# Attention with a softplus feed-forward on one core: q and k of the first three units loaded head-major and transposed in bf16

## The chip, the cores and the metric

The kernel runs on one core of one Trainium2 chip, in one launch. The metric is the device time in microseconds (us) from start to end; 218.96 us is the median of three runs of the kernel before (218.79 to 218.98). The profile is of one execution, which took 219.03 us.

## The reference

Two stages. Attention over 4 sequences of 768 tokens with 8 heads of 64; a query sees the 8 first tokens and its last 96, with a bias by distance. Then, for each of 3072 tokens, a feed-forward of 512 to 2048 to 512 with softplus.

```python
scores = scale * np.matmul(q, k.transpose(0, 1, 3, 2))
keep = is_global | is_local            # pos < 8, or 0 <= rel < 96
scores = np.where(keep, scores + bias, -1e9)
a = softmax(scores)
x = np.matmul(a, v)                    # to [tokens, heads * 64]
h = x @ w_in
g = np.maximum(h, 0.0) + np.log1p(np.exp(-np.abs(h)))
out = g @ w_out
```

## The kernel before, in words

**Tiling.** A block is 128 tokens of a sequence; a unit is two blocks (`UNITS`, L204: twelve units, twenty-four blocks). A unit's q, k and v are loaded as float32 (512 KB each), cast to bf16, and q and k are transposed so that the 64 features of a head lie on partitions. Of a block's scores, TensorE computes key tile by query (L1005 for the first block, L1058 for the others), the bias is added on TensorE (L995, L1039, for the first two blocks) or on VectorE (L1084), ScalarE exponentiates (L1018, L1091), TensorE multiplies with v and a column of ones (L1110), VectorE divides (L1121, L1122), and the result is transposed to `XT` (L1141 on TensorE for the first six blocks, by a DMA after that). Two blocks make a group of 256 tokens: `mm1` (L1168, eight slots of eight matmuls) writes h, ScalarE computes exp and ln(1+e) (L1183, L1194), `mm2` (L1217) multiplies with w_out, and `store` copies and writes out (L1246, L1249).

**The first three units** (`WIDE`, L205: units 0, 1 and 2) have a path of their own for q and k. Each of these six tensors is loaded in two DMAs of 256 KB, one for the even heads and one for the odd heads (L780 to L783): 128 partitions of 2 KB, eight tokens of one head in each. Partition number is token group times four plus head (`"h (g r) d -> g h (r d)"`). The first q is issued on ScalarE's queue (`LOAD_ON`), all other loads on SyncE's. `cast_q` (L841) casts each half, 128x512. `transp_pe` (L914 to L947) transposes on TensorE by a matmul with the identity (L926): the output is float32 in PSUM, and because heads alternate from partition to partition, each matmul scatters its 128 columns over the bank with a stride. One q or k of a unit has eight such matmuls and fills two banks. Then either one copy of 1024 columns (L939) or two of 512 (L936) bring it to bf16 in `qT` or `kTa`/`kT`. The other nine units are loaded whole (L790 to L793), and a DMA transposes them (L953).

**Weights** come in sixteen loads of 512 KB (L821), eight of w_in and eight of w_out, and are cast to bf16 (L823).

**What sets the order.** Each piece of work is an `op` with an engine, an assumed duration and a due time. `Planner.run` (L90) plays the pieces through a model of the engines and of the transfers (constants `FETCH`, `DMA_FIRST`, `DMA_LAST` and the pair `dma=(work, packet)` of an op) and fixes the order on each engine; the instructions are then written out in this order. `NUDGE` shifts due times of single ops, `CHOICE` gives the engine of an op that could run on several. So the constants do not appear in the instructions; they decide where these stand. `filler` (L1330) makes 35 matmuls on a blank tile, written where the planner sees TensorE without work. On the chip each engine goes through its list in order and waits on semaphores.

Of the kernel before, what the change touches and what calls it, by code (L numbers as in the profile page):

```python
# [23 lines left out]
class Planner:  # L24
# [5 lines left out]
    FETCH = 15.5  # L30
    FETCH_COST = 1.0
    DMA_FIRST = 0.75
# [182 lines left out]
    0: (("s", 1, 0), ("s", 1, 1), ("s", 0, 0), ("s", 0, 1)),  # L215
    1: (("s", 1, 0), ("s", 1, 1), ("s", 0, 0), ("s", 1, 0)),
    2: (("s", 0, 0), ("s", 1, 0), ("s", 1, 0), ("s", 0, 0)),
# [48 lines left out]
    "a0.0": -2,  # L266
    "a0.1": -14.5,
    "a0.2": -3,
    "a0.4": 2.25,
    "a1.0": -1,  # L270
    "a1.1": -4.25,
    "a1.2": -3.5,
    "a1.3": -0.5,
    "a1.4": 0.5,
    "a1.6": 15,
    "a1.7": -2,
    "a2.0": 8,
    "a2.2": -11,
    "a2.3": 1.5,
    "a2.4": 4,  # L280
    "a2.5": -10.25,
    "a2.6": -4,
    "a2.7": 8,
    "b0.0.2": 10.5,
    "b0.0.4": -8.5,
    "b0.0.8": -8,
    "b0.1.0": 0.5,
    "b0.1.10": -7.5,
    "b0.1.12": -14.75,
    "b0.1.14": 2.75,  # L290
    "b0.1.2": -1,
    "b0.1.4": 3.75,
    "b0.1.6": -40.75,
    "b0.1.8": 2.75,
    "b1.0.0": 4.75,
    "b1.0.10": 4.5,
    "b1.0.12": -11,
    "b1.0.14": -2,
    "b1.0.2": 1,
    "b1.0.4": -0.5,  # L300
    "b1.0.8": -18.25,
    "b1.1.0": 4.25,
    "b1.1.10": -0.5,
    "b1.1.12": 0.25,
    "b1.1.4": 0.5,
    "b1.1.6": 10,
    "b1.1.8": 55.75,
    "biasFalse0": 2.25,
    "biasFalse2": -2,
    "biasFalse4": 5.5,  # L310
    "biasFalse5": -6.75,
    "biasFalse6": 10,
    "biasFalse7": -5.25,
    "biasTrue0": 1.75,
    "biasTrue2": -2,
    "biasTrue3": 2,
    "biasTrue4": -4,
    "biasTrue6": -0.5,
    "biasTrue7": -1.5,
    "blank": -7,  # L320
    "castk0.0": -2.25,
    "castk0.1": -11.25,
    "castk1.1": 11.5,
    "castk2.0": 4,
    "castk2.1": -8.25,
    "castk3.00": 4.5,
    "castk3.01": -2.5,
    "castk3.10": -0.25,
    "castk3.11": 1,
    "castk4.00": 3.5,  # L330
    "castk4.11": -0.25,
    "castq0.1": 23.25,
    "castq1.1": 16,
    "castq2.0": -17.25,
    "castq2.1": 1.5,
    "castq3.0": 7,
    "castq5.0": 9,
    "castv0.01": 3.5,
    "castv0.10": -1.25,
    "castv0.11": 3,  # L340
    "castv1.00": -13.5,
    "castv1.01": 4,
    "castv1.10": 4,
    "castv1.11": -4.5,
    "castv2.00": 6.5,
    "castv2.01": 8,
    "castv2.10": 8.5,
    "castv2.11": 1.25,
    "castv3.00": 0.75,
    "castv3.10": 0.25,  # L350
    "castv3.11": -20,
    "castv4.00": 1,
    "castv4.10": 0.25,
    "castv4.11": -8,
    "castv6.10": -0.5,
    "castv6.11": -8,
    "cin1": -10,
    "cin2": -3.25,
    "cin3": -67.25,
    "cin4": -0.5,  # L360
    "cin5": -6,
    "cin6": -0.25,
    "cin7": 29,
    "cout0": -6.75,
    "cout1": -19.5,
    "cout3": 0.75,
    "cout4": 2.5,
    "cout6": 6,
    "cout7": -3.25,
    "cpk0.0": -2.75,  # L370
    "cpk1.0": 20.25,
    "cpk1.1": 6.75,
    "cpk2.0": -2,
    "cpk2.1": 9,
    "cpq0.0": 7.25,
    "cpq1.0": -1.25,
    "cpq2.0": 3,
    "d0": -4.25,
    "dl0a": -0.25,
    "dl0b": -0.25,  # L380
    "dl0c": -0.25,
    "dl1a": 0.5,
    "dl1e": 2.5,
    "e0.1": 3.75,
    "e0.2": -4,
    "e0.3": -18.75,
    "e0.4": -1,
    "e0.6": -0.5,
    "e1.0": -2,
    "e1.1": 2,  # L390
    "e1.2": -23,
    "e1.3": 12.5,
    "e1.5": 0.5,
    "e1.6": -1,
    "e1.7": -9.75,
    "e2.3": 2.75,
    "e2.4": -0.5,
    "e2.5": 11.25,
    "ex0.0": 0.75,
    "ex0.1": -8,  # L400
    "ex2.0": -67.75,
    "ex2.1": 2.25,
    "ex3.0": 6.5,
    "ex3.1": -1.5,
    "ex4.0": -23.5,
    "ex4.1": 3.75,
    "ex5.0": -0.25,
    "ex5.1": -26,
    "ex6.0": 0.5,
    "ex6.1": 8.5,  # L410
    "ex7.0": 23.75,
    "ex7.1": 3.75,
    "gk4": 0.5,
    "gk6": 11.75,
    "gk8": 12,
    "gv4.0": -0.75,
    "gv4.1": 1.25,
    "gv5.0": -1,
    "gv5.1": 12,
    "gv6.0": 7,  # L420
    "gv6.1": -6,
    "gv7.1": 0.25,
    "gv8.0": -8,
    "gv8.1": 1,
    "ident": 9.75,
    "iota": -1,
    "ldk0.0": -2,
    "ldk0.1": -6.25,
    "ldk1.0": -5.25,
    "ldk2.0": 0.25,  # L430
    "ldk2.1": 26,
    "ldk3": -4,
    "ldk4": 10.5,
    "ldk5": 1.75,
    "ldq0.0": 1,
    "ldq0.1": 23,
    "ldq1.1": -4,
    "ldq2.0": 12.5,
    "ldq2.1": -4.25,
    "ldq3": -4,  # L440
    "ldv0": 13,
    "ldv3": -8.75,
    "ldv4": -9.5,
    "ldv5": 4,
    "ldv6": -2,
    "ldv7": 16.75,
    "ldv8": 8,
    "ln0.0": 16.5,
    "ln0.2": 4.75,
    "ln0.3": -8.5,  # L450
    "ln1.0": -15,
    "ln1.2": 2,
    "ln2.0": -177.75,
    "ln2.1": 8.75,
    "ln2.2": -8,
    "nm1.0": -12,
    "nm2.0": 7.25,
    "nm2.1": 1,
    "nm3.0": -1,
    "nm3.1": -1,  # L460
    "nm5.0": 2,
    "nm6.0": -12,
    "nm6.1": 1,
    "oc0.0.0": 4,
    "oc0.1.0": 30.25,
    "oc1.0.0": -8,
    "pv0.0": 12,
    "pv0.1": -17.75,
    "pv1.0": -4,
    "pv1.1": 1.25,  # L470
    "pv2.0": 12,
    "pv2.1": -13.75,
    "pv3.0": 0.25,
    "pv3.1": 5.5,
    "pv4.1": 1,
    "pv5.0": -4,
    "pv5.1": 1,
    "pv6.0": 3,
    "pv6.1": -3.25,
    "sb0.0": 2.25,  # L480
    "sb1.1": 17.5,
    "sc0.0": -8,
    "sc1.0": 8,
    "sc1.1": 7.75,
    "sc2.0": 0.5,
    "sc3.0": 9,
    "sc4.0": 7.25,
    "sc5.1": 2,
    "sc6.0": 0.5,
    "sc7.0": -2.25,  # L490
    "st0.0.0": 7.25,
    "st0.1.0": -0.25,
    "st1.0.0": 1,
    "table": -3,
    "trk0.0": 1.5,
    "trk1.0": 1.5,
    "trk1.1": 72.5,
    "trk2.0": -24.5,
    "trk2.1": 1.5,
    "trk4": -2.5,  # L500
    "trq0.0": -36.5,
    "trq1.0": 2,
    "trq2.0": 4,
    "trq2.1": 0.5,
    "trq3": 0.25,
    "trq5": 0.25,
    "win1": -0.5,
    "win5": -16,
    "win6": 1,
    "wout0": -12.5,  # L510
    "wout1": -1.75,
    "wout2": -18.5,
    "wout4": 3.75,
    "wout5": 2,
    "wout7": -11.75,
    "xc1": 5.25,
    "xc2": 1,
    "xc3": 1.75,
    "xc4": 0.25,
    "xc5": -6.5,  # L520
    "xt1": 2,
    "xt2": -82.5,
    "xt4": 5.25,
    "xt5": -2,
    "xt6": -6.75,
    "z2.0": 0.25,
    "z3.0": -8.25,
    "z4.0": -2,
    "z4.1": 15,
    "z5.0": -2,  # L530
    "z6.0": 8,
    "z6.1": -47.25,
# [22 lines left out]
    "biasFalse0": "POOL",  # L555
    "biasFalse2": "DVE",
    "biasFalse5": "DVE",
    "biasTrue0": "DVE",
    "biasTrue1": "DVE",
    "biasTrue2": "DVE",  # L560
    "biasTrue3": "POOL",
# [5 lines left out]
    "castk2.0": "POOL",  # L567
    "castk3.00": "ACT",
    "castk3.01": "ACT",
    "castk3.10": "DVE",  # L570
    "castk3.11": "ACT",
    "castk4.00": "DVE",
    "castk4.01": "ACT",
    "castq0.0": "POOL",
# [3 lines left out]
    "castq4.0": "POOL",  # L578
    "castq5.0": "POOL",
    "castv0.00": "DVE",  # L580
    "castv0.01": "POOL",
    "castv0.10": "ACT",
    "castv1.00": "DVE",
    "castv1.01": "POOL",
    "castv1.10": "DVE",
    "castv2.11": "ACT",
    "castv3.00": "ACT",
    "castv3.01": "DVE",
    "castv3.10": "ACT",
    "castv3.11": "DVE",  # L590
    "castv4.01": "ACT",
    "castv4.10": "ACT",
    "castv4.11": "ACT",
    "cin1": "ACT",
    "cin3": "DVE",
    "cin5": "DVE",
    "cin6": "DVE",
    "cout3": "ACT",
    "cout6": "DVE",
    "cout7": "DVE",  # L600
    "cpk0.0": "DVE",
    "cpk1.1": "ACT",
    "cpk2.1": "DVE",
    "cpq0.0": "ACT",
    "cpq2.1": "ACT",
    "gk4": "ACT",
    "gk5": "ACT",
    "gk6": "ACT",
    "gk7": "ACT",
    "gv4.0": "ACT",  # L610
    "gv4.1": "ACT",
    "gv5.0": "ACT",
    "gv6.0": "DVE",
    "gv8.0": "DVE",
    "oc0.0.0": "ACT",
    "xc1": "ACT",
    "xc4": "ACT",
# [13 lines left out]
def kernel(  # L631
# [116 lines left out]
    def held(keys):  # L748

        return sorted({key[:2] for key in keys})  # L750
# [13 lines left out]
    def load_unit(i, rank, only="qkv"):  # L764
# [4 lines left out]
        for z, which in enumerate(only):  # L769
# [4 lines left out]
            if i in WIDE and which != "v":  # L774
                for y in range(2):

                    on = LOAD_ON.get(f"{which}{i}", "SP")

                    def fn(src=src, raw=raw, y=y, on=on):
                        return dma_on[on].dma_start(  # L780
                            raw[:, 512 * y : 512 * y + 512],
                            src[y::2, sl, :].rearrange("h (g r) d -> g h (r d)", r=8),
                        )  # L783

                    op(f"ld{which}{i}.{y}", on, 0.64, rank + 0.01 * z, fn, dma=(0.68, 86.0), sync=sync,
                       writes=[("raw", slot, y)])
                continue
# [7 lines left out]
            op(f"ld{which}{i}", "SP", 0.45, rank + 0.01 * z, fn, dma=(2.5 if (which, i) == ("v", 0) else 1.8, 30.0), sync=sync,  # L795
# [84 lines left out]
    def q_of(n):  # L880
# [3 lines left out]
        if i in WIDE:  # L884
            return lambda rows, m: t[rows, NPAIR * x + m, :]
# [5 lines left out]

    def kt_unit(i):
        name, slot = kt_tile(i)
        return {"kTa": kTa, "kT": kT}[name][slot][:]
# [605 lines left out]
```

## Time and profile before

| | |
|---|---|
| median of three runs | 218.96 us |
| profiled execution | 219.03 us, its span 217.2 us: 1.83 us lie outside the span |
| TensorE matmul (PE) busy | 211.7 us, 97% |
| ScalarE (ACT), VectorE (DVE), GpSimd (POOL) busy | 170.7, 115.7, 74.4 us |
| granted TensorE clock | 0.998 |
| DMA | 40.95 MB, mean 188 GB/s; 333 to 387 GB/s in the slices from 5 to 38 us |

The page is in parts: busy time of each engine; the span in 40 equal slices of 5.43 us, as tenths of busy time; DMA queues; the chain of work that ended last; the costliest groups of instructions, by line of the kernel; and DMA issues. In rows of a timeline the first number is the start, the second the time from the start of the row's first instruction to the end of its last, and xN counts instructions merged into the row. Matmuls overlap: the time that a run of matmuls takes from TensorE is read from the start of one row to the start of the next.

### The profile page before, as it was taken

To read this page: it belongs to the slowest core of one execution; us is meant where nothing else is said; L and a number is where in the kernel's file an instruction comes from. 1 tells how busy PE (TensorE), PEld (TensorE's weight loads), DVE (VectorE), ACT (ScalarE), POOL (GpSimd) and SP (SyncE) were. 2 spreads that over 40 slices of the span, in tenths; PEclk is the share of its full clock that TensorE was granted. 3 is DMA by queue.
4 is the path that set the end of the run, shared out by engine and by line. 5 is a ranking of instruction groups with operands and counts; after the bars stand their busy time and mean duration, and the time that the engine had idled before them with its cause. 6 is when DMAs were issued, how large, how long until landed. Compare 5 with 4: busy or idle time off the path is not lost.

```text
span 217.2 us, 4970 instructions
## 1 busy us (share of the span) xinstructions
PE 211.7 (97%) x2003; PEld 144.5 (67%) x2003; DVE 115.7 (53%) x216; ACT 170.7 (79%) x236; POOL 74.4 (34%) x127
## 2 busy tenths in 40 slices
PE   7899999999999999999999999999999999999994
PEld 2576887656665787757767767756766767767554
DVE  6568868674489667327546546446545952101121
ACT  4899999999995699978788688678697878788300
POOL 6316333253059525900265274233236320000000
PEclk9999999999999999999999999999999999999999
DMA  5999999999999399945895996892687212011112
GB/s 202 333 367 387 386 357 367 317 286 214 225 317 175 104 236 264 211 108 155 147 231 160 159 218 165 207 165 72 127 209 198 69 30 75 0 48 53 48 48 97
DMA packets 69846, 40.95 MB, mean 188 GB/s; under 512 B 30144, under 2 KB 61248, under 8 KB 69824
## 3 DMA queue, kind: packets, MB, share of 16 engines
q1 hardware_dynamic: 69392, 40.05, 72.1%
q10 hardware_dynamic: 432, 0.59, 0.9%
q8 instruction: 15, 0.25, 0.5%
q14 instruction: 7, 0.06, 0.1%
HBM read 27.26 MB, written 6.29 MB: 154 GB/s over the span
## 4 chain that ended last, share of the span: by engine, by line
PE 83%; ACT 12%; DMA 2%; issue 2%; SPq 0%; DVE 0%
PE h_ps L1168 34%; PE o_ps L1217 30%; PE s_ps L1058 5%; PE x_ps L1110 4%; ACT pb L1091 3%; ACT e L1183 3%; PE s_ps L1217 3%; PE s_ps L926 2%; DMA raw<-in_k_dram 2%; PE x_ps L1217 2%; ACT g L1194 2%; PE x_ps L1330 1%; ACT vb L976 1%; ACT XT L1146 1%; ACT kb L865 1%
## 5 line engine op out<-in xcount | busy, mean ns | idle before, releaser
L1168 PE MATMUL h_ps<-XT,w_in_bf 128*128 128x256 bf16 x768 | 95.8, 273 | 0.9 <-ACT e L1183 0.7
L1168 PEld LDWEIGHTS <-w_in_bf 128*128 128x128 bf16 x768 | 73.6, 98 | 18.7 <-issue 1.7
L1217 PE MATMUL o_ps<-w_out_bf,g 128*128 128x512 bf16 (+1 forms) x320 | 77.7, 371 | 0.0
L1183 ACT ACTIVATE e<-h_ps 128x512 f32<-128x512 f32 x96 | 59.5, 627 | 20.9 <-PE h_ps L1168 20.5
L1217 PEld LDWEIGHTS <-g 128*128 128x128 bf16 x416 | 37.3, 98 | 28.6
L1084 DVE TENSOR_TENSOR z<-s_ps,biasA 128x1024 f32<-128x1024 f32 x38 | 45.8, 1219 | 15.2 <-PE s_ps L1058 8.6
L1194 ACT ACTIVATE g<-e 128x1024 bf16<-128x1024 f32 x48 | 50.7, 1057 | 1.3
L1091 ACT ACTIVATE pb<-z 128x1024 bf16<-128x1024 f32 (+1 forms) x44 | 43.1, 988 | 7.9 <-DVE z L1084 7.9
L1246 DVE COPY osb<-o_ps 128x512 f32<-128x512 f32 (+1 forms) x20 | 13.4, 670 | 37.1 <-PE o_ps L1217 37.1
L976 POOL COPY vb<-vb 4x512 bf16<-4x512 bf16 x27 | 16.4, 608 | 33.0 <-PE x_ps L1110 28.6
L865 POOL CAST vb<-raw 64x512 bf16<-64x512 f32 x33 | 20.4, 617 | 18.0 <-DMA raw<-in_v_dram 16.8
L865 POOL CAST kb<-raw 64x512 bf16<-64x512 f32 x30 | 18.6, 619 | 19.5 <-DMA raw<-in_k_dram 18.4
L1110 PEld LDWEIGHTS <-pb 128*128 128x128 bf16 x352 | 16.5, 98 | 6.1 <-ACT pb L1091 0.2
L1122 DVE TENSOR_TENSOR xs<-x_ps,rcp 128x256 bf16<-128x256 f32 x40 | 17.0, 424 | 1.4
L1121 DVE RECIPROCAL rcp<-x_ps 128x4 f32<-128x4 f32 x40 | 7.2, 179 | 18.7 <-PE x_ps L1110 18.3
L1110 PE MATMUL x_ps<-vb,pb 128*128 128x65 bf16 x304 | 15.9, 193 | 0.0
L1217 PE MATMUL s_ps<-w_out_bf,g 128*128 128x512 bf16 (+1 forms) x64 | 13.6, 352 | 0.0
L1330 PE MATMUL x_ps<-blank 128*128 128x512 bf16 x35 | 11.1, 442 | 1.2 <-DVE blank L1269 1.2
L1058 PEld LDWEIGHTS <-kT 64*128 64x128 bf16 x224 | 6.8, 94 | 5.1 <-issue 4.9
L1058 PE MATMUL s_ps<-qT,kT 64*128 64x128 bf16 x224 | 9.9, 218 | 0.0
L1084 DVE TENSOR_TENSOR z<-s_ps,bias 128x512 f32<-128x512 f32 x6 | 3.9, 687 | 7.3 <-PE s_ps L1058 7.3
L1246 ACT COPY osb<-x_ps 128x128 f32<-128x128 f32 x1 | 0.3, 266 | 8.7 <-PE x_ps L1217 8.7
(84 smaller groups left out, 120.7 us busy)
## 6 DMA issues: line engine op xcount, KB each, us to landing
raw<-in_v_dram SPq DMA_DIRECT2D x12, 512.0 KB, 5.7
out_dram<-osb SPq DMA_DIRECT2D x23, 256.0 KB, 2.3
raw<-in_q_dram SPq DMA_DIRECT2D x9, 512.0 KB, 4.5
raw<-in_k_dram SPq DMA_DIRECT2D x9, 512.0 KB, 5.6
raw<-in_moe_w_in_dram SPq DMA_DIRECT2D x8, 512.0 KB, 9.5
raw<-in_moe_w_out_dram SPq DMA_DIRECT2D x8, 512.0 KB, 8.6
raw<-in_k_dram SPq DMA_DIRECT2D x6, 256.0 KB, 6.0
raw<-in_q_dram SPq DMA_DIRECT2D x4, 256.0 KB, 8.0
```

Source lines behind the costliest of these rows:

```text
L865: copy_on[eng](dst, src)
L976: copy_on[eng](vb_of(prev)[sl, :, 0:D], vb_of(first)[sl, :, 0:D])
L1058: nc.tensor.matmul(reg if unit_of(n) in WIDE else reg.rearrange("p (r t) -> p r t", r=2), kt[rows, 2 * part + m, :], qv(rows, 2 * part + m ...
L1084: nc.vector.tensor_tensor(z, src, bias, ALU.add)
L1091: nc.scalar.activation(pb[:, 0:nr, :].rearrange("p (y a) b -> p y (a b)", y=2), src, AF.Exp, scale=1.0 / root_d)
L1110: nc.tensor.matmul(xv[:, h, :], pb[:, 4 * (h % 2) + 2 * part + h // 2 if lone else u_all * (2 * (h % 2) + h // 2) + u, :], vb_of(prev if u ...
L1122: nc.vector.tensor_tensor(xs[:, 4 * part : 4 * part + 4, :], xv[:, :, 0:D], rcp[:][:, :, None].to_broadcast([P, 4, D]), ALU.mult,)
L1168: last = nc.tensor.matmul(hv[:, j, :], w_in_bf[:, m, fb * P : fb * P + P], XT[g % NXG][:, m, :], start=(m == 0), stop=(m == NM - 1),)
L1183: nc.scalar.activation(e[:, p % 2, :, :].rearrange("p j (b t r) -> p (j b) r t", b=2, r=2), hb[:].rearrange("p (a r t) -> p a r t", a=4, r=2),
L1194: nc.scalar.activation(gt[:, 2 * p - 2 : 2 * p + 2, :].rearrange("p a t -> p (a t)"), e[:].rearrange("p a j t -> p (a j t)"), AF.Ln, bias=1.0,
L1217: nc.tensor.matmul(bank(key)[:, 0 : z - a], gt[:, fb, ns * P : ns * P + P], w_out_bf[:, fb, a:z], start=(fb == 0), stop=(fb == NFB - 1),)
L1246: copy_on[eng](osb[:, a:z], bank(key)[:, 0 : z - a])
```

## The change

**Loads.** The halves of q and k of units 0 to 2 keep their size, number and 2 KB rows; partition number is now head times 32 plus token group. On the DRAM side the outermost dimension of the transfer was 32 token groups and is now 4 heads; on the SBUF side it stays 128 partitions.

**Transposes.** Eight transposes per q or k as before, but with a bf16 result of 128 contiguous columns each, so that one q or k fills one bank and not two. They stand as one op (`PE_KEYS` names one bank, not up to four).

**Copies out.** Always two copies of 512 columns; each reads PSUM with a stride of 128 columns and writes 64 columns in a row. In `qT` and `kTa`/`kT` a wide unit's head pairs and blocks change places, which `q_of`, `kt_unit` and `globals_k` follow.

**Planner.** `FETCH` 15.5 to 18.0, `DMA_FIRST` 0.75 to 0.62, the assumed work of the first v load 2.5 to 1.8, the assumed duration of the table load 1.3 to 0.1; new `NUDGE` and `CHOICE` tables. The assumed work of a wide half (0.68) stays.

What comes of it in the instruction lists: 48 transposes, 35 fillers, 768 matmuls of `mm1` and all other matmuls are as many as before. The lists' order to the last transposes of q (unit 2) is another, but what stands ahead of them on TensorE is the same in number: 64 matmuls of mm1, 48 of L1110, 48 of scores, 16 of L1141, all fillers; ahead of them in addition, now, the eight of k of unit 2, which stood behind. SyncE's loads, before: k0 k0, v0, q1 q1, k1, w_in, k1, v1, seven w_in, q2 q2, k2 k2, three w_out, v2, four w_out, q3, k3, w_out. After: k0 k0, q1, v0, q1, w_in, k1, two w_in, k1, w_in, v1, four w_in, k2 k2, q2 q2, three w_out, v2, four w_out, q3, k3, w_out. On ScalarE's queue both halves of q0 in both.

```diff
-    FETCH = 15.5
+    FETCH = 18.0
-    DMA_FIRST = 0.75
+    DMA_FIRST = 0.62
...
 PE_KEYS = {
-    0: (("s", 1, 0), ("s", 1, 1), ("s", 0, 0), ("s", 0, 1)),
-    1: (("s", 1, 0), ("s", 1, 1), ("s", 0, 0), ("s", 1, 0)),
-    2: (("s", 0, 0), ("s", 1, 0), ("s", 1, 0), ("s", 0, 0)),
+    0: (("s", 0, 0), ("s", 1, 0)),
+    1: (("s", 1, 0), ("s", 0, 0)),
+    2: (("s", 0, 0), ("s", 1, 0)),
 }
...
                             raw[:, 512 * y : 512 * y + 512],
-                            src[y::2, sl, :].rearrange("h (g r) d -> g h (r d)", r=8),
+                            src[y::2, sl, :].rearrange("h (g r) d -> h g (r d)", r=8),
                         )
...
-            return lambda rows, m: t[rows, NPAIR * x + m, :]
+            return lambda rows, m: t[rows, 2 * m + x, :]
...
+    def kT_t(i):
+        name, slot = kt_tile(i)
+        return {"kTa": kTa, "kT": kT}[name][slot]
+
     def kt_unit(i):
-        name, slot = kt_tile(i)
-        return {"kTa": kTa, "kT": kT}[name][slot][:]
+        t = kT_t(i)[:]
+        return t.rearrange("p x m t -> p (x m) t").rearrange("p (m x) t -> p x m t", x=2) if i in WIDE else t
...
-    def transp_pe(i, which, banks, engs, rank):
+    def transp_pe(i, which, key, engs, rank):
...
+        tr = bank(key).bitcast(BF16)
+
+        def mm():
+            for r in range(2):
+                for a in range(4):
+                    c, z = P * (2 * a + r), P * (4 * r + a)
+                    nc.tensor.transpose(tr[:, z : z + P], src[:, c : c + P], ident[:])
+
+        op(f"tr{which}{i}.0", "PE", 0.45, rank, mm, count=8,
+           reads=[(which + "b", i % NQB, x) for x in range(4)] + ["ident"], writes=held([key]))
+        for r in range(2):
+
+            def ev(eng, r=r):
+                copy_on[eng](
+                    dst[:, :, 64 * r : 64 * r + 64].rearrange("p c (g a) -> p c g a", a=4),
+                    tr[:, 512 * r : 512 * r + 512].rearrange("p (a c g) -> p c g a", a=4, g=16),
+                )
...
-        dst = kt_of(prev).rearrange("p m (r t) -> p (m r) t", r=2)[:, :, 0:GH]
-        src = kt_of(first).rearrange("p m (r t) -> p (m r) t", r=2)[:, :, 0:GH]
+        dst = kt_of(prev).rearrange("p m (r t) -> p m r t", r=2)[:, :, :, 0:GH]
+        src = kt_of(first).rearrange("p m (r t) -> p m r t", r=2)[:, :, :, 0:GH]
...
-    op("table", "ACT", 1.3, TABLE_RANK, table, writes=["table"])
+    op("table", "ACT", 0.1, TABLE_RANK, table, writes=["table"])
```

## The prediction, as made before the changed kernel was run

> **What bounds the kernel now.** I read the page's busy times first, then the waits of TensorE, then its timeline. TensorE is busy 97% of the span and waits for others three times, 2.5 us in all:
>
> ```profile
> PE 211.7 (97%) x2003; PEld 144.5 (67%) x2003; DVE 115.7 (53%) x216; ACT 170.7 (79%) x236; POOL 74.4 (34%) x127
> ...
> DMA  5999999999999399945895996892687212011112
> GB/s 202 333 367 387 386 357 367 317 286 214 225 317 175 104 236 264 211 108 155 147 231 160 159 218 165 207 165 72 127 209 198 69 30 75 0 48 53 48 48 97
> ```
>
> ```profile
> PE x_ps L1330 <- DVE blank L1269: 1.2, 1, 1.2
> PE h_ps L1168 <- ACT e L1183: 0.7, 2, 0.4
> PE s_ps L926 <- ACT kb L841: 0.6, 1, 0.6
> ```
>
> So the time is TensorE's list laid end to end, plus what holds it up. That list includes 35 fillers. What the fillers cover is the wait for data: in the same stretch the transfers run flat out (DMA row: 9 of 10 from the second slice on, to 387 GB/s). An earlier end needs fewer us of TensorE work; a later end comes from data that arrive later than TensorE's list asks for them, and here the DMA has no slack to make up with.
>
> The rows of TensorE that the working uses (start, us, ..., count):
>
> ```profile
> 6.79 1.05 PE L926 MATMUL s_ps<-ident,kb 128*128 128x128 bf16 x8 [0.62 <-ACT kb L841]
> 7.63 1.08 PE L926 MATMUL s_ps<-ident,qb 128*128 128x128 bf16 x8
> ...
> 15.97 0.43 PE L1141 MATMUL h_ps<-ident,xs 128*128 128x128 bf16 x4
> 16.24 1.03 PE L1330 MATMUL x_ps<-blank 128*128 128x512 bf16 x4
> ```
>
> ```profile
> 29.24 1.04 PE L926 MATMUL s_ps<-ident,qb 128*128 128x128 bf16 x8
> ```
>
> Eight old transposes take 7.63 - 6.79 = 0.84 us of TensorE, 0.105 each. Four bf16 transposes with contiguous output (L1141) take 16.24 - 15.97 = 0.27; at the other places of that line 0.23. I use 0.0575 each. From the transposes of q of unit 2 (29.24) to the end of the span lie 217.2 - 29.24 = 187.96 us, all of it TensorE's list and its tail.
>
> The transfers, in stretches (the last two columns are the mean share of the 16 DMA engines and GB/s):
>
> ```profile
> 2.00:3.00 1.00, 1.00 (x4) 0.44 (x3) 0.88 (x4) 0.67 (x1) 0.47 (x3) 1.00 0.68 156
> 3.00:4.00 1.00, 1.00 (x4) 0.29 (x3) 0.92 (x6) 0.11 (x1) 0.31 (x2) 1.00 1.03 385
> 4.00:5.00 1.00, 1.00 (x4) 0.36 (x3) 0.90 (x6) 0.50 (x2) 0.94 (x2) 1.00 1.05 402
> ...
> 6.00:7.00 1.00, 0.38 (x4) 0.21 (x4) 0.00 (x0) 0.88 (x3) 0.20 (x1) 1.00 1.12 324
> ...
> 20.00:25.00 5.00, 4.64 (x54) 4.08 (x52) 4.47 (x10) 4.95 (x8) 1.63 (x3) 1.00 1.05 387
> ```
>
> From 3 to 4 us only halves of k0 and q0 can be in flight, and all sixteen engines are full: 385 GB/s, 24 for each engine.
>
> **The transposes and copies.** 48 transposes save 0.0475 each, 2.28 us of TensorE: 1.06 ahead of the point at 29.24 (32 old ones, 3.36, against 40 new, 2.30) and 1.22 behind it (16 old, 1.68, against 8 new, 0.46). All other matmuls and the fillers are as many on both sides of this point. Where TensorE is never short of data, all 2.28 us are gain.
>
> Copies out: two of 512 in place of one of 1024 or two of 512. The rows:
>
> ```profile
> L939 ACT CAST qT<-s_ps 128x1024 bf16<-128x1024 f32 x2 | 2.0, 1012 | 0.3 <-PE s_ps L926 0.3
> ...
> L936 DVE CAST kT<-s_ps 128x512 bf16<-128x512 f32 x2 | 1.4, 691 | 0.7 <-PE s_ps L926 0.7
> ...
> L936 ACT CAST kTa<-s_ps 128x512 bf16<-128x512 f32 x2 | 1.1, 589 | 0.0
> ...
> L1146 DVE COPY XT<-o_ps 128x512 bf16<-128x512 bf16 x2 | 0.8, 416 | 0.4 <-PE o_ps L1141 0.4
> ```
>
> A copy that reads bf16 with a stride is not in the trace. Bounds: 0.42 on DVE (contiguous bf16) and, twice the float32 row, 1.38. I take the float32 rows, 0.69 and 0.59: ACT takes 0.57 for contiguous bf16 too, and the 0.27 that DVE gains there may go with the stride. Then two copies on two engines cost about 0.7 where one of 1024 cost 1.0 to 1.2; ACT and DVE have gaps there, and fillers stand on TensorE (5 after the first transposes before, 7 now), so this is worth nothing at the end. At 1.38 it would cost 0.7 on the path of each q and k, bounded under the rivals. The moved casts and biases land on engines that, in the forecast below, wait for data anyway: nothing. The four-dimensional copies of the global keys (32 elements, about 0.2 us) and the planner's constants: nothing.
>
> **The loads: the large term.** The size, rows and issue costs stay; what changes is the outermost dimension on the DRAM side, 32 token groups before, 4 heads after. A transfer must be dealt out to sixteen engines. Every load of the kernel before has an outermost size that sixteen divides on both sides (32, or 128 for v and the weights, to 128 partitions), and the rows show all sixteen busy; none shows what happens with 4. Bounds: still sixteen engines, 262,144 B / 387 GB/s = 0.68 us a half; or one engine per head, four engines, each moving 65,536 B at 24.2 GB/s: 2.71 us. I take 2.71: dealing out whole outermost items is the simplest rule that fits the rows, and with it four items cannot occupy more than four engines. I also take it that these are the same four every time, since nothing in the code steers it.
>
> Beside this stands a rule: the Trainium skill, page "DMA: Bandwidth & Descriptors", section "Why a DMA increments its semaphore by 16 and not by 1", says that a transfer runs on the largest number of engines up to 16 that divides the slowest dimension of both sides, and on HWDGE on the lowest-numbered ones. By it 32 and 128 give 16, with which the trace agrees (385 GB/s), and 4 and 128 give 4, the forecast's case; no run so far shows the second.
>
> Then those four engines are the queue that everything passes through, because every other transfer also has a sixteenth of its bytes on each of them. Work on each of the four up to the last half of q2, in SyncE's new order: 12 halves x 2.71 = 32.5; 8 w_in of 524,288 B at 387 GB/s, 1.35 each, 10.8; v0 and v1 in 512 B rows (row 6 to 7 us, 324 GB/s), 1.62 each, 3.2. Sum 46.5 us, against 12 x 0.68 + 14.0 = 22.2 before. Start: 156 GB/s in the third us means 0.4 us at full rate, so 2.6. The last half of q2 is in at 49.1. From last byte to cast: k0a and q0a (524 KB) were moved by 3.96 (156 KB by 3.0, the rest at 385 GB/s), and the first cast of k started at 4.70: 0.74. The cast of this half stands on POOL, 0.72 (723 ns); TensorE follows 0.05 later (6.74 to 6.79). So the transposes of q2 start at 49.1 + 0.74 + 0.72 + 0.05 = 50.6.
>
> Nothing ahead of them on TensorE is later: the eighth w_in is in after 12 - 4 = 8 halves, 21.7 + 10.8 + 3.2 = 35.7, at 38.3, cast (1.12 on POOL) by 40.2, and k2 (two halves later) at 44.5. Behind them: 187.96 - 1.22 = 186.7 us. The last w_out needs 8 x 1.35 + 3 x 1.62 = 15.7 more, so 66.6 with landing and cast; TensorE's new list asks for it some 17.7 us after the transposes (68.3). It holds by under 2 us, so I add no stall, but up to 5 us above.
>
> Sum: 50.6 + 186.7 = 237.3, and 219.03 - 217.2 = 1.83 outside the span: 239.1 us. The profiled execution is 0.07 above the median, which I neglect. **Predicted: 239.1 us**, 20 us slower.
>
> **The rivals.**
>
> *Sixteen engines all the same: faster.* If the cut reaches inside a head, halves take 0.68 us. Then the list is 2.28 us shorter, and the two stalls of about 0.5 us at 21.8 and 26.75 may or may not go: 217.2 - 2.28 = 214.9, with 1.83 outside 216.8 us (215.8 without the stalls). It holds up to about 0.8 us a half: the queue then ends at 2.6 + 14.0 + 12 x 0.8 = 26.2, and with 1.5 for landing and cast q2 is there at 27.7; TensorE reaches its transposes at 29.24 - 1.06 = 28.2, or 0.5 sooner. For it: nothing in the rows excludes it, the DRAM bytes are contiguous. Against: it needs a cut within an item.
>
> *Sixteen engines, but strided copies at twice the price.* Each of unit 0 and 1's copies adds 0.7 to TensorE's start of scores, k after q on both engines: 2 x 1.4 = 2.8 beyond the fillers. 216.8 + 2.8 = 219.6, about no change or slightly slower. For: before, a stride on TensorE's own output doubled its time (0.105 against 0.0575). Against: ACT's 0.57 and 0.59 for bf16 and float32 show a price that goes by elements.
>
> *Four engines, but other ones for each transfer.* The total then spreads, only the time of one transfer grows by 2.03. Halves overlap, and units 0 and 1 are each later by about one such step: 214.9 + 2 x 2.03 + 1.83 = 220.8.
>
> **How the numbers follow.** Four common engines 0.80 (239.1); sixteen, fine 0.11 (216.8, faster); sixteen with slow copies 0.05 (219.6: slower 0.03, same 0.01, faster 0.01); four changing ones 0.04 (slower 0.03, same 0.01). Faster by over 0.2%, about what a measurement of this kernel can tell, 0.12; same 0.02; slower 0.86. The range for the first case: at 402 GB/s the queue is 1.7 us shorter, and if the four engines, alone on the memory, move up to 10% more than a sixteenth of the full rate, 5 us: 232. At 324 GB/s the queue is 9 us longer, with 5 for w_out and unit 3: 253. So 232 to 253, which with 0.80 for its case is the 8 in 10; the faster case lies outside.
>
> **What would show it.** Right: slices of the first 49 us at about 180 GB/s (8.4 MB in 46.5 us) in place of 333 to 387; halves of q and k landing far over 10 us after issue; TensorE waiting ahead of the transposes of k1 and q2, for casts that waited for DMA; the row of q2's transposes at about 50.6, eight in 0.46 us; from there on TensorE as dense as before. Wrong: 380 GB/s from 3 us on and the transposes of q2 at 27 to 29, which is the faster rival. Copies of 512 at over 1 us would show the second rival.

## The result, and the profile after

The changed kernel takes **246.43 us** (median of five runs, 245.95 to 247.14), the kernel before 218.96 (218.79 to 219.36): a ratio of 1.1257, 95% interval 1.1233 to 1.1280. The forecast was 239.1 us, 232 to 253: the side is right and the time lies in the range, but the loss is 27.5 us where 20 were forecast. The profiled execution has a span of 244.9 us, so 1.8 us lie outside it, as before. All ratios here are of fast executions; the longest execution of experiments 3 and 8 counts as slow, so it is in their medians and not in their ratios.

The page, TensorE's busy time, the granted clock and the transfers by slice (now 6.1 us each):

```profile
PE 218.7 (89%) x1974; PEld 146.8 (60%) x2003; DVE 115.7 (47%) x220; ACT 167.5 (68%) x227; POOL 79.7 (33%) x135
...
PEclk9858776995999999999999999999999999999999
...
GB/s 52 153 152 206 216 258 192 217 205 308 277 305 220 272 242 204 116 218 287 179 81 143 262 147 211 144 157 257 95 130 175 193 64 24 64 43 15 32 86 86
```

The first nine slices (55 us) move 52 to 258 GB/s, 183 on average; before, 333 to 387 stood from 5 to 38 us. The granted clock is below nine tenths in slices 2 to 7 (6 to 43 us) and in slice 10 (55 to 61 us), and nowhere else.

The windows of after, three rows (the last three columns are the granted clock, the share of the 16 DMA engines and GB/s):

```profile
5.00:6.00 1.00, 1.00 (x4) 0.44 (x3) 0.48 (x2) 0.00 (x0) 0.92 (x2) 1.00 0.26 100
...
20.00:25.00 5.00, 2.18 (x22) 0.83 (x17) 0.00 (x0) 2.03 (x5) 1.87 (x3) 0.99 0.82 217
...
55.00:60.00 5.00, 3.79 (x22) 2.90 (x23) 2.49 (x4) 4.18 (x7) 0.69 (x1) 0.50 0.82 288
```

From 5 to 6 us the first halves of q and k are moving (v0, whose issue ends at 6.99, shows from 8 us on): 0.26 of 16 is 4.2 engines, with 24 GB/s each. The same row of before, in which v0 is already moving, has 1.05 and 326 GB/s. From 20 to 25 us weights move beside the halves: 13.1 engines are busy, but with 16.5 GB/s each.

The waits of TensorE, the longest three, and its timeline around the transposes of k2 and q2:

```profile
PE h_ps L1001 <- ACT bias L1312: 5.9, 1, 5.9
PE s_ps L939 <- ACT qb L851: 5.5, 1, 5.5
PE s_ps L939 <- DVE rcp L1127: 3.5, 2, 1.9
```

```profile
49.05 0.61 PE L939 MATMUL s_ps<-ident,kb 128*128 128x128 bf16 x8 [1.62 <-DVE rcp L1127]
49.50 0.38 PE L1147 MATMUL o_ps<-ident,xs 128*128 128x128 bf16 x4
...
56.21 1.01 PE L939 MATMUL s_ps<-ident,qb 128*128 128x128 bf16 x8 [5.45 <-ACT qb L851]
57.10 3.57 PE L1174 MATMUL h_ps<-XT,w_in_bf 128*128 128x256 bf16 x16
60.60 0.29 PE L1064 MATMUL s_ps<-qT,kT 64*128 64x128 bf16 x2
```

The releasers named are on the compute engines, but the one that matters was late itself: the cast `qb` that releases the transposes at 56.21 had waited 7.78 us for `raw<-in_q_dram`. The transposes of k2 take 49.50 - 49.05 = 0.45 us, those of q2, after 5.45 us of idle TensorE, 0.89. From 57 us to the end no wait is listed: the delay is complete by then.

### The profile page after: what moved, and what is told of

Its sections match the earlier page's. It is cut to its first block, busy times and chain, and to the rows that moved or that the text cites. A ratio compares the mean times of both kernels' runs of the same rounds, so it can differ in the third digit from the quotient of the medians.

```text
span 244.9 us, 4949 instructions
## 1 busy us (share of the span) xinstructions
PE 218.7 (89%) x1974; PEld 146.8 (60%) x2003; DVE 115.7 (47%) x220; ACT 167.5 (68%) x227; POOL 79.7 (33%) x135
## 4 chain that ended last, share of the span: by engine, by line
PE 73%; DMA 14%; SPq 10%; issue 1%; DVE 0%; ACT 0%; POOL 0%; ACTq 0%; POOLq 0%
PE h_ps L1174 31%; PE o_ps L1223 26%; DMA raw<-in_q_dram 7%; SPq L790 5%; DMA raw<-in_v_dram 5%; PE s_ps L1223 5%; PE x_ps L1116 4%; PE s_ps L1064 4%; SPq L831 3%; DMA XT<-xs 2%; PE x_ps L1223 2%; SPq L800 2%; PE s_ps L939 0%; ACT qb L851 0%; POOL vb L875 0%
## 5 line engine op out<-in xcount | busy, mean ns | idle before, releaser
L1174 PE MATMUL h_ps<-XT,w_in_bf 128*128 128x256 bf16 x768 | 98.5, 278 | 0.2
L1174 PEld LDWEIGHTS <-w_in_bf 128*128 128x128 bf16 x768 | 74.4, 100 | 18.8 <-DMA XT<-xs 0.3
L1223 PE MATMUL o_ps<-w_out_bf,g 128*128 128x512 bf16 (+1 forms) x295 | 73.6, 371 | 1.2
L875 POOL CAST vb<-raw 64x512 bf16<-64x512 f32 x38 | 24.2, 637 | 26.7 <-DMA raw<-in_v_dram 25.4
L875 POOL CAST kb<-raw 64x512 bf16<-64x512 f32 x32 | 19.8, 620 | 20.4 <-DMA raw<-in_k_dram 19.2
L1336 PE MATMUL x_ps<-blank 128*128 128x512 bf16 x33 | 13.8, 581 | 1.4 <-DVE blank L1275 1.2
L1223 PE MATMUL s_ps<-w_out_bf,g 128*128 128x512 bf16 (+1 forms) x62 | 13.0, 352 | 0.1
L851 ACT CAST qb<-raw 128x512 bf16<-128x512 f32 x4 | 2.5, 616 | 11.0 <-DMA raw<-in_q_dram 11.0
L1336 PEld LDWEIGHTS <-blank 128*128 128x128 bf16 x35 | 4.4, 137 | 7.1 <-issue 5.5
```

What stands on the lines that cost most here:

```text
L875: copy_on[eng](dst, src)
L1174: last = nc.tensor.matmul(hv[:, j, :], w_in_bf[:, m, fb * P : fb * P + P], XT[g % NXG][:, m, :], start=(m == 0), stop=(m == NM - 1),)
L1223: nc.tensor.matmul(bank(key)[:, 0 : z - a], gt[:, fb, ns * P : ns * P + P], w_out_bf[:, fb, a:z], start=(fb == 0), stop=(fb == NFB - 1),)
L1336: nc.tensor.matmul(x_ps[:], blank[:, 0:P], blank[:])
```

## The experiments

Theory: a half whose outermost DRAM dimension is 4 runs on four engines, the same four each time, and q2's last half sets when the dense part of TensorE's list may begin. Rivals: the new order of the work or the strided copies cost the time; head-major partitions cost it whatever the number of engines. The trace of after adds a question: where halves follow one another they land every 3.1 to 3.3 us and not every 2.71. (A landing time, here and below, is that of the last of a load's landing events in the trace; the page has none for these loads.)

### 1. The loads back

```diff
-                            src[y::2, sl, :].rearrange("h (g r) d -> h g (r d)", r=8),
+                            src[y::2, sl, :].rearrange("h (g r) d -> g h (r d)", r=8),
...
-                    dst[:, :, 64 * r : 64 * r + 64].rearrange("p c (g a) -> p c g a", a=4),
-                    tr[:, 512 * r : 512 * r + 512].rearrange("p (a c g) -> p c g a", a=4, g=16),
+                    dst[:, :, 64 * r : 64 * r + 64].rearrange("p (h x) (g a) -> p h x g a", x=2, a=4),
+                    tr[:, 512 * r : 512 * r + 512].rearrange("p (a x g h) -> p h x g a", a=4, x=2, g=16),
```

> The changed kernel with one thing undone: the halves of q and k are loaded with token groups outermost again (32 on the DRAM side); the copies out read PSUM with four strides to sort the columns. The instruction order is that of the changed kernel. Theory A, the loads run on four engines because the outermost size is 4: landing times of the halves fall back to 3 to 8 us, the transposes of q2 start at 27 to 29 us, and the time is 216.8 us (215.8 to 218.5), below before. Theory B, the loss comes from the rest of the change (strided copies, new order, casts on other engines): the time stays near 246.

Measured: 218.21 us (217.61 to 219.59), ratio to before 0.9967 (0.9947 to 0.9988). The bf16 transposes, the two copies of 512 (with one more stride), the order and the planner's constants are all in it, so the 28 us go with the loads. It is 1.4 us above the expected 216.8. Its timeline of unit 0's copies shows one candidate:

```profile
7.22 0.69 DVE L946 COPY qT<-s_ps 128x512 bf16<-128x512 bf16 x1 [1.74 <-PE s_ps L939]
7.95 0.59 ACT L946 COPY qT<-s_ps 128x512 bf16<-128x512 bf16 x1 [0.23 <-DVE qT L946]
8.43 0.59 ACT L946 COPY kTa<-s_ps 128x512 bf16<-128x512 bf16 x1
9.05 0.69 DVE L946 COPY kTa<-s_ps 128x512 bf16<-128x512 bf16 x1 [1.14 <-ACT kTa L946]
```

The durations are those of the float32 rows, 0.69 and 0.59: the stride costs nothing that these rows can show. But the second copy of a pair begins when the first has ended, so a pair takes 8.54 - 7.22 = 1.32 us.

### 2. The loads alone

The kernel before, with the head-major loads, and the scatter of its old transposes set to match.

```diff
-                            src[y::2, sl, :].rearrange("h (g r) d -> g h (r d)", r=8),
+                            src[y::2, sl, :].rearrange("h (g r) d -> h g (r d)", r=8),
...
-                    tr = bank(banks[r]).rearrange("p (x m g a) -> p a x g m", x=2, m=NPAIR, a=4)
+                    tr = bank(banks[r]).rearrange("p (x m g a) -> p a m x g", x=2, m=NPAIR, a=4)
```

> The kernel before with the loads alone changed: heads outermost (4), and the scatter of the float32 transposes permuted to match; order, copies and all else are those of before. Theory A: the four engines get 24 us more work by the end of q2, so the transposes of q2 and k2 move from 29 to about 56 us and the time is 243 to 249 us. Theory B: the loads alone cost nothing, 219 us.

Measured: 244.87 us (244.45 to 245.70), ratio 1.1189 (1.1165 to 1.1212). With experiment 1 this closes it from both sides: the loads alone bring 25.7 us over the 219.13 of before in the same comparison, everything else without them -0.9. The two add up to 24.8, and after loses 27.5: the last 2.7 us come only where both meet, and no run takes them apart. The two longest waits of TensorE are for casts of k, which in turn wait for DMA (9.6 us on ScalarE, 16.9 on GpSimd, for `raw<-in_k_dram`); a third, of 4.8 us, is put down to `rcp`:

```profile
PE s_ps L926 <- ACT kb L841: 9.3, 1, 9.3
PE s_ps L926 <- POOL kb L841: 5.0, 1, 5.0
```

### 3. Eight items in place of four

Before, with a half made of eight heads by 128 tokens in place of four heads by 256, head outermost. Features and tokens land in the wrong places, so the scores are not those of the reference; the work on every engine is the same.

```diff
-                            src[y::2, sl, :].rearrange("h (g r) d -> g h (r d)", r=8),
+                            src[:, P * b0 + P * y : P * b0 + P * y + P, :].rearrange("h (g r) d -> h g (r d)", r=8),
```

> The kernel before, with each half of q and k now one block of all 8 heads in place of two blocks of every other head: same bytes, same 2 KB rows, outermost size 8 on the DRAM side. The features then land in the wrong places, so what is computed is not the reference's; the work of every engine is as before. Theory A: eight engines, 1.35 us a half and 12 x 0.68 = 8 us more work on these eight by q2 and k2; before had about 3 us to spare there; time 223 to 227 us. If what counts is only whether a head's rows lie together in DRAM or partitions: as slow as with 4 outermost, 243 to 249 us. Theory B: 219 us.

Measured: 230.08 us (228.65 to 232.91), ratio 1.0479 (1.0443 to 1.0515); the profiled execution is the longest. The windows of it, from 3 to 4 us, when only halves are moving:

```profile
3.00:4.00 1.00, 1.00 (x4) 0.30 (x2) 0.92 (x6) 0.32 (x2) 0.32 (x2) 1.00 0.47 166
```

0.47 of 16 is 7.5 engines with 22 GB/s each. So the outermost dimension counts the engines: 32 items 219.1 us, 8 items 230.1, 4 items 244.9. The time for 8 is 3 us above what had been expected, which would fit halves that cost more than bytes by engines; experiment 5 looks at that.

### 4. Fillers in q2's wait

After, with 24 more fillers just ahead of the transposes of q2.

```diff
+            if (which, i) == ("q", 2):
+                for _ in range(24):
+                    nc.tensor.matmul(x_ps[:], blank[:, 0:P], blank[:])
```

> The changed kernel with 24 more filler matmuls on TensorE just ahead of the transposes of q2, where it stood idle for 5.45 us. If the 2.0 us that the rest took longer than forecast came from the lower clock after the idle time (16 matmuls of mm1 took 3.50 us right after it, 1.75 elsewhere): the 16 take about 1.75 and the time falls by 1.5 to 2 us to about 244.7. If they were slow because data came late: 246.4, no change. If the fillers themselves end late: slower.

Measured: 245.61 us (244.61 to 246.39), ratio 1.1207 (1.1180 to 1.1235), beside 1.1257 (1.1233 to 1.1280) for after: 0.8 us less by the medians, 1.1 by the ratios, where 1.5 to 2 had been expected, and the two intervals just touch. Its timeline:

```profile
55.97 0.61 PE L942 MATMUL s_ps<-ident,qb 128*128 128x128 bf16 x8
56.87 2.06 PE L1177 MATMUL h_ps<-XT,w_in_bf 128*128 128x256 bf16 x16 [0.29 <-ACT XT L1155]
58.85 0.23 PE L1067 MATMUL s_ps<-qT,kT 64*128 64x128 bf16 x2
```

The sixteen matmuls of mm1 take 58.85 - 56.87 = 1.98 us where after needs 60.60 - 57.10 = 3.50. So the slow start after q2's wait is the granted clock (0.50 in after's row of 55 to 60 us, 1.00 here) and not the data. At 61 us this kernel is 1.95 us ahead of after; at 97 it is 0.6 us ahead, having waited 0.34 us at 79.65 for an exponential and 0.57 at 95.79 for a copy of kT, which after does not. Its span is 244.2 us, 0.7 less than after's: most of the lead is given back, two thirds of the loss in these two waits.

### 5. The halves without weights beside them

After, with all halves of q and k, and v0 and v1, issued ahead of the first weight.

```diff
-FIRST_LOADS = "k0 q0 v0 i3 i1 q1 k1 o0 i0 i2 i4 v1 i6 o1 i7 q2 k2 i5 o4 o5 o2 o3 o6 o7 v2".split()
+FIRST_LOADS = "k0 q0 v0 q1 k1 v1 q2 k2 i3 i1 o0 i0 i2 i4 i6 o1 i7 i5 o4 o5 o2 o3 o6 o7 v2".split()
...
-           writes=raw_keys(slot), dma=cost)
+           writes=raw_keys(slot), dma=cost, after=[o for o in pl.ops if o.name.startswith(("ldq2", "ldk2"))])
```

> The changed kernel with one edit: all ten later halves of q and k (and v0, v1) are issued ahead of the first weight load, so that the halves run with almost no transfer on 16 engines beside them. It is not meant to be a fast kernel: the weights come late. Read from it when the last half of q2 lands, and the time of one packet. Theory one (a half on four engines is 2.71 us when it is alone, and the 3.1 us seen is what the shares of the 16-engine transfers on the same four engines add): packets near 84 ns, a half every 2.7 to 2.8 us, last half landed at about 38.6 us. Theory two (3.1 us a half is what four engines need here, whoever runs beside them): packets near 100 ns, last half at about 44.6 us, which is 55.4 less the 10.8 us of the eight weight loads. Time of the kernel: 245 to 260 us by either, since TensorE then waits for weights.

Measured, one profiled run: 252.77 us; the last of the twelve halves lands at 39.31 us (expected 38.6 by the first theory, 44.6 by the second). While nothing runs beside the halves they land at 21.71, 24.30, 26.88 and 29.46: 2.58 us each. Its windows, halves alone and then with v1 beside:

```profile
21.00:26.00 5.00, 3.75 (x42) 1.91 (x41) 0.61 (x2) 4.04 (x7) 0.34 (x1) 1.00 0.28 105
29.00:33.00 4.00, 0.00 (x0) 0.00 (x0) 0.00 (x0) 0.00 (x0) 0.00 (x0) 0.56 0.72 181
```

Alone, 4.5 engines with 23.4 GB/s each; with a 16-engine load beside them, 11.5 with 15.7. A packet of 2 KB takes 84 ns in the trace while halves run alone, as the first theory expected; in after it takes 127 to 130 ns on average from 20 to 24 and from 48 to 55 us. So 2.58 us is the price of a half alone, and what comes on top in after goes with the transfers that run beside it. But it is not their shares on the four engines, as the first theory had it: in after the first w_out's last four shares land from 55.78 us on, behind q2, and the halves of k2 and q2 ahead of them still take 2.51, 3.69, 3.96 and 2.96 us. So the four engines themselves are slower, 20 GB/s each on average (65,536 B in 3.28 us) in place of 25 (in 2.58). Here too the last three halves, with v1 and weights beside them, take 3.29 us each. Why an engine moves less then, these runs don't show.

### 6. The transposes alone

Before, with the bf16 transposes and the strided copies of experiment 1, and with before's tables for order and engines.

```diff
-                        nc.tensor.matmul(tr[:, a], src[:, c : c + P], ident[:])
+                    nc.tensor.transpose(tr[:, z : z + P], src[:, c : c + P], ident[:])
...
+                    dst[:, :, 64 * r : 64 * r + 64].rearrange("p (h x) (g a) -> p h x g a", x=2, a=4),
+                    tr[:, 512 * r : 512 * r + 512].rearrange("p (a x g h) -> p h x g a", a=4, x=2, g=16),
```

> The kernel before with the transposes alone: bf16 to contiguous PSUM columns, eight for one tile, and two strided copies out; loads, nudges and engine choices as before. The prediction's terms (48 transposes save 2.28 us, copies cost nothing): 216.8 us. The rival formed since (the second copy of a pair is issued only when the first has ended, so that a pair costs about 1.3 us and not 0.7, and TensorE waits for kT at the first scores): 0.6 to 1.5 us of the 2.28 come back, 217.5 to 218.5 us. Slower than 219.5 would say that the copies cost more than the transposes save.

Measured: 220.04 us (218.71 to 220.86), ratio 1.0035 (1.0012 to 1.0058): slower than before, and above both expectations. TensorE is busy 1.1 us less (210.6), but beside the constant 1.2 for the blank tile it waits 3.5 us, in eight places of at most 0.7, where before waited 1.3; none of them is for the transposes or for the two copies of 512. Experiment 1 differs from this in the tables, the planner's constants and so the order; that is worth 1.5 to 1.8 us (by the ratios and by the medians).

### 7. Pairs of copies that don't wait for each other

Experiment 1, with the halves of a q or k transposed to two PSUM tiles, and the destination indexed by half.

```diff
-        tr = bank(key).bitcast(BF16)
+        trs = [bank(("s", r, key[1])).bitcast(BF16) for r in range(2)]
...
-                    dst[:, :, 64 * r : 64 * r + 64].rearrange("p (h x) (g a) -> p h x g a", x=2, a=4),
+                    dst.rearrange("p (h x) (r g a) -> p r h x g a", x=2, r=2, a=4)[:, r],
```

> The changed kernel with the loads back in token groups (as the first experiment, 218.2 us), and the two copies of a tile made free of each other: the two halves of the transposes go to two PSUM tiles, and the destination is indexed by half and not sliced. In the built program the pairs of q0, k2 and q2 then wait for TensorE alone; that of k0 still runs one after the other. If serial copies were what kept the first experiment at 218.2 where 216.8 was expected: 217.0 to 217.7 us. If the rest was lost elsewhere (order, later waits for data): 218.0 to 218.4 us, as the first experiment.

Measured: 218.07 us (217.20 to 219.71), ratio 0.9949 (0.9925 to 0.9973). The copies of q0 now overlap:

```profile
8.20 0.58 ACT L946 COPY qT<-s_ps 128x512 bf16<-128x512 bf16 x1 [0.26 <-PE s_ps L939]
8.42 0.69 DVE L946 COPY qT<-s_ps 128x512 bf16<-128x512 bf16 x1 [2.55 <-PE s_ps L939]
```

The median stands 0.14 us below that of experiment 1, the profiled execution 1.6 us in span. Both kernels were run again, side by side:

> The kernel of the first experiment once more (the changed kernel with its loads in token groups), so that it stands on the same chip in the same call as the kernel with the freed pairs of copies. Both theories expect 218.2 us again (217.6 to 218.8).

> The kernel with the freed pairs of copies once more, beside the one that it is compared with. In the two profiled runs its TensorE list was 1.7 us earlier from 23 us to the end; the medians of two different calls differ by 0.14 us only. If the freed copies are worth what the two traces show: 0.8 to 1.7 us below its neighbour, and 216.5 to 217.4 us. If the profiled run of the neighbour was an odd one and the freed copies are hidden: within 0.4 us of it.

Measured: 218.41 us (217.53 to 218.86; ratio 0.9963, 0.9944 to 0.9981) with the serial pairs, 218.54 (217.26 to 219.56; ratio 0.9967, 0.9947 to 0.9987) with the freed ones: no difference. In these two traces the freed kernel reaches k2's transposes at 27.42 us, the serial one at 28.57; then it loses 1.7 us in one place (waits of TensorE):

```profile
PE s_ps L1064 <- POOL kT L972: 1.7, 1, 1.7
```

So serial copies cost about 1 us at 28 us, and in this pair of runs nothing at the end: the lead went into a wait for a small copy on POOL. Whether that wait would go with another order was not tried.

### 8. Head-major partitions on all engines

After, with each half loaded by four transfers, one for a head, whose outermost dimension is 32 token groups.

```diff
-                        return dma_on[on].dma_start(
-                            raw[:, 512 * y : 512 * y + 512],
-                            src[y::2, sl, :].rearrange("h (g r) d -> h g (r d)", r=8),
-                        )
+                        for x in range(4):
+                            last = dma_on[on].dma_start(
+                                raw[32 * x : 32 * x + 32, 512 * y : 512 * y + 512],
+                                src[2 * x + y, sl, :].rearrange("(g r) d -> g (r d)", r=8),
+                            )
+                        return last
```

> The changed kernel with its head-major partitions kept, but each half is loaded by four transfers, one for a head, whose outermost dimension is 32 token groups. Theory (what costs is the outermost dimension of 4, not where the data land): the loads run on 16 engines again, part 6 shows a landing time for them, GB/s over 300 in the first 30 us, no gap of more than 2 us before the transposes of k1 and q2. Price of the edit itself: some 30 more issues at about 0.6 us on SP put the issue of q2's last piece at about 31 us, its landing at 33, q2's transposes at about 35 and the end at about 223 us (219 to 226). Rival (head-major partitions or the layout of the raw tile cost by themselves): 235 us or more.

Measured: 230.74 us (228.71 to 234.04), ratio 1.0473 (1.0417 to 1.0529): 16 us below after, and 5 us outside what had been expected. The sixteen engines are back (slices of 216 to 372 GB/s from 6 to 29 us). Most of what is left is the price of the edit, in SyncE's timeline (start, length, issues):

```profile
22.82 8.99 SPq L791 DMA_DIRECT2D raw<-in_k_dram  x8
31.91 4.67 SPq L791 DMA_DIRECT2D raw<-in_q_dram  x8
```

An issue takes 0.58 to 1.12 us here, not 0.6 throughout, so the issue of q2's last piece ends at 36.6 and not at 31, and q2's transposes start at 38.81 and not at 35. Just behind them the list is 8.1 us behind experiment 1 (39.70 against 31.61); 1.3 us more go into the first sixteen mm1 (3.30 us, not 1.99, after a wait of 2.3), and some 1.5 by 62 us, where a wait for w_out (0.9) is the longest. Where the data land is not what costs; on how many engines they come is. One transfer with token groups outermost and head-major partitions would need to step over partitions within a transfer; it was not tried.

## Why the prediction was right in its mechanism and short by 7 us

**What bounds the kernel: right.** TensorE's list, with nothing between, from the transposes of q2 on. The stretch forecast at 186.7 us is 217.6 - 31.08 = 186.5 in experiment 1, 186.6 in its second run, and 216.0 - 29.11 = 186.9 with the freed copies; in the second run of those it is 217.8 - 28.96 = 188.8, with the 1.7 us wait of experiment 7 in it. (The prediction counts three waits in the kernel before; its rows show four, which changes no sum.)

**Four engines, the same four: right.** 100 GB/s and 4.2 busy engines when halves are alone. The trace's landing events show the same: a half of after has one event right after its issue and four later; a weight load behind has twelve early and four late (the first w_in by 18.93 and at 25.00). Here the rule cited in the prediction is borne out (the Trainium skill, page "DMA: Bandwidth & Descriptors", section "Why a DMA increments its semaphore by 16 and not by 1"): the largest number up to 16 that divides both slowest dimensions, with the issuer counting the missing engines at once. The DRAM sides of 32, 8 and 4 items gave 16, 7.5 and 4.2 busy engines.

**The queue on the four: the term that was too small.** Forecast 46.5 us from 2.6 to 49.1, and 49.84 with 0.74 for landing. q2's last half landed at 55.37: 5.5 us later. The failed step is "one engine per head, four engines, each moving 65,536 B at 24.2 GB/s: 2.71 us", used for every half: 2.58 when alone (experiment 5), but in after 11.75 us for the first four (2.6 to 15.09, less 0.74 for landing; 2.94 each, with v0 on the other engines for a part of it), 8.8 for q1 and v0 (to 23.88; 7.0 by the terms), and 13.1 for k2 and q2 (42.25 to 55.37, 3.28 each, with w_out on the other twelve). The stretch between, k1, eight w_in and v1, took 0.5 us more than its terms. The range had such a rate (324 GB/s, 20 an engine, 9 us longer); the value taken did not: it assumed that an engine moves as much when the others work beside it.

**Landing to transposes: right.** 0.84 us (55.37 to 56.21), forecast 0.77.

**Behind q2, 186.7: short by 2.0.** 244.9 - 56.21 = 188.7. The step took TensorE at full clock from its first instruction on. After 5.45 us of idling, the eight transposes took 0.89 and the sixteen mm1 3.50, where experiment 1 has 0.53 and 1.99: 1.9 us.

```profile
31.61 2.06 PE L1174 MATMUL h_ps<-XT,w_in_bf 128*128 128x256 bf16 x16
33.60 0.23 PE L1064 MATMUL s_ps<-qT,kT 64*128 64x128 bf16 x2
```

The granted clock was 0.50 there. The Trainium skill says the same, page "TensorE: Matmul & The Clock Gate", section "Part 1: The HAM clock gate (the "warmup" mystery)": after an idle window of some 3.4 us the clock is halved; the trace agrees, with a granted 0.50 in the row of 55 to 60 us, after 5.45 us of idling. The forecast had TensorE wait for q2, but not this consequence.

From the second sixteen mm1 (start at 61.36 us in after, 34.15 in experiment 1) to the last mm1, after needs as long as experiment 1 (169.1 us both), so the slow start accounts for nearly all of the 2.0. It is not what a full clock would save: experiment 4, with the clock at 1.00, ends only 0.7 us earlier in its span, since later waits take up most of the lead.

Sum: 239.1 + 5.5 + 0.1 + 2.0 = 246.7, the profiled run's 244.9 + 1.8. That the range held both was in part luck: it had a slower rate, but nothing for the clock, and its 5 us for w_out and unit 3 went unused.

**"Nothing ahead of them on TensorE is later": right in effect.** TensorE waited earlier too (5.9 us for a bias at unit 0, 3.5 at k1 and k2), but each wait ended ahead of q2's data. These are the same late halves: the bias stands on ScalarE behind a cast that waited 8.29 us for k, and the last halves of k1 and k2 landed at 33.99 and 48.45, 0.60 ahead of their transposes. k2 came at 48.45, four us later than forecast, by the same short term. The w_out margin of 2 us held: no wait after 57 us.

**The transposes: right in size, wrong in worth.** 0.45 us for eight, 0.056 each (forecast 0.0575). That its stride alone made the old transpose cost twice as much is not shown: the old ones also had a float32 result, and no run changes one without the other. And "where TensorE is never short of data, all 2.28 us are gain" failed: experiment 1 kept 0.7 to 0.9 of it, and with before's tables none was left (experiment 6, ratio 1.0035). TensorE is busy 1.1 us (experiment 6) and 1.7 us (experiment 1) less, and waits some 2 us more.

**The copies: price right, sum wrong.** 0.69 and 0.59, as taken; the rival with a doubled price falls. But "two copies on two engines cost about 0.7" is 1.32, since one runs after the other. That this costs nothing at the end holds in the medians (experiment 7), but not for the reason given: at 28 us the serial copies cost 1 us in spite of the fillers, and in the one pair of traces a later wait took it back.

**The rivals.** Sixteen engines, fine or with slow copies, fall with the 100 GB/s; other engines for each transfer falls with the w_in loads, whose last four shares land 6 us behind the twelve others.

## What to carry to other kernels

Read the outermost dimension of every transfer before reordering it: with 4 in place of 32 on the DRAM side the kernel took 28 us more for the same bytes and rows, and splitting the transfer to get the engines back still left 12 of them, most through late issues. A transfer on few engines is paid twice, by itself and by every full-width transfer that has shares queued behind it, so price it as a queue on those engines, and with what an engine moves when its neighbours work, not when it is alone. Where the forecast has TensorE idle for several us, add the half-speed restart (1.9 us here, of which fillers in the gap won back about 0.8 at the end); and count us saved on a full engine as gain only up to the next datum that it has to wait for.

## What the runs showed of the hardware that was not expected

An engine that moves 23 to 24 GB/s with halves alone moves 15.7 to 16.5 when 16-engine loads run beside (after, 20 to 25 us; experiment 5, 29 to 33 us), though before had all sixteen at 24 together. A part of the second row is v1 with its rows of 512 B, which move at 20 GB/s an engine in before, too; from 20 to 24 us the packets are of 2 KB. The cause stays open.

The issue of a load can hold SyncE for up to 7 us while halves are queued on the four engines. That a full queue is what holds it is likely, but not shown. In after:

```profile
2.97 4.02 SPq L800 DMA_DIRECT2D raw<-in_v_dram  x1
7.04 6.97 SPq L790 DMA_DIRECT2D raw<-in_q_dram  x1
```

Before, the same two issues took 0.61 and about 0.7 us. So the first weight load is issued at 14.05 us, not at 5.08, and twelve engines have nothing to do from 11.5 to 14 us (0.26 of the engines, 98 GB/s).
